# Head pairs and dense products in 64-row halves of the array, attention chunk by chunk, x turned up front

## The chip, the cores and the metric

The kernel runs on one core of a Trainium2 chip. The metric is the device time of one execution in microseconds. Three executions of the kernel before took 794.4, 798.03 and 798.63 us; the median is 798.03 us. Engine names follow the profile: PE is TensorE (PEld its weight loads), DVE is VectorE, ACT is ScalarE, POOL is GpSimd, SP is SyncE, whose queue issues every DMA here.

## The reference

One token matrix `x` of 2048 x 512 goes through two branches, and a gate mixes them:

```python
g = sigmoid((x * gate_w).sum(-1, keepdims=True))
# A: 32 heads of 16, causal window of 256
q, k, v = split(x @ wqkv)
scores = q k^T * 16**-0.5, masked to 0 <= i - j < 256
a = (softmax(scores) v) @ wo
# B: 512 -> 1792 -> 512
b = gelu_tanh(x @ w1 + b1) @ w2 + b2
return g * a + (1 - g) * b
```

## The kernel before

**Arithmetic.** Dense products keep fp32 accuracy with three passes. Each operand is split into a high part and a low remainder, and one product of 128 x 128 by 128 x 512 becomes three matmuls, high by high, high by low and low by high (`mm3`, L90 to L92). A score product uses one pass instead: the high and low parts of a head are stacked as extra rows of the contraction (48 rows for each of two heads, `load_stack`, L341 and L342), so that a single matmul sums the three terms.

**Tiles.** Tokens are cut in four tiles (chunks) `t` of 512. `x` arrives in 128-token blocks, is turned by four 128 x 128 transposes on PE (L198) and kept as `xt`. The query, key and value products (`qkv_qk`, `qkv_v`; 12 groups of 12 matmuls for each tile) are written to DRAM (`SQ`, `SK`, `SV`) and read back in the stacked layout (`att_load`). The other branch has 56 groups `u` of 12 matmuls (`x @ w1`, then `gelu`, L535 to L553) and 32 groups `y` of 21 matmuls (`@ w2`, L601). `final` multiplies the attention output by `wo`: 192 matmuls of full width at the end.

**Attention.** Heads go in 8 groups `g_` of 4, and keys in 16 blocks `kb` of 128. For each block and head there are two score products of up to 384 columns. The first (`att_max`, L377) feeds the row maximum on DVE (L382). The negated maxima are turned and put by POOL into spare rows of the query stack (`att_rows`, L402), so that the second product (`att_exp`, L417) comes out with the maximum subtracted; ACT takes its exponential (L429) and POOL cuts the window edges (L421, L424). Every four blocks, `att_pv` (L449) multiplies the probabilities by the values, with four heads side by side in 32-column quarters of the array.

**Order of the work.** PE, ACT, DVE and POOL run in the order in which the program is written. A small planner (`tick`, `after`, `need`) places the follow-up operations by estimated times. One unit of attention is one key block of four heads: four `att_max`, four `att_exp`, and a share of dense work of `STEP` = 2296 ns between them (`fill`), taken as single `mm3` triples. The unit loop goes head group by head group, 16 blocks each, with the maxima 8 units ahead of the exponentials (`LEAD`). Before it stand 117 us of planned dense work (`START`): three tiles of query, key and value products and part of the fourth. SP's order is not written out. It is arranged when the program is built: an issue whose inputs are ready can move ahead of those that wait.

Of the kernel before, what the change touches and what calls it, by code (L numbers as in the profile page):

```python
# [18 lines left out]
T = 512  # L19
# [5 lines left out]
NG = H // 4  # L25
SCALE = DH ** -0.5
NEG = -1e30
GC = 1.0 / 0.044715
GS = 0.7978845608028654 * 0.044715


@with_exitstack
def gated_mix(ctx: ExitStack, tc: tile.TileContext, x, wqkv, wo, w1, b1, w2, b2, gate_w, out):
# [21 lines left out]
    XT = [dr.tile([NC, 128, 2, T], F32, name=f"XT{t}") for t in range(NT)]  # L55
# [5 lines left out]

# [12 lines left out]
    own = cp.tile([128, 4], F32, name="own")  # L74
    nil = cp.tile([128, 1], F32, name="nil")
    nc.gpsimd.memset(nil, 0.0)
    nc.gpsimd.memset(own, 0.0)
    for k in (0, 1):
        nc.gpsimd.affine_select(out=own[96:104], in_=own[96:104], pattern=[[-2, 4]], compare_op=ALU.not_equal,
                                fill=1.0, base=-k, channel_multiplier=1)  # L80
    nms = cp.tile([128, RB, 32], F32R, name="nm")
    nc.gpsimd.memset(f32(nms), 0.0)
    vbuf = cp.tile([128, 2, NB * 68 + 16], F32, name="vbuf")
    nc.gpsimd.memset(vbuf[:, :, NB * 68:], 0.0)
# [8 lines left out]

# [23 lines left out]

    wk4 = wqkv.rearrange("(c p) f -> p c f", p=128)
    wt, raws = {}, {}

    def load_raw(key, early=False):
# [6 lines left out]
        if early and kind == "v":  # L128
            if i == 0:
                raws["v"] = f32(sb.tile([128, NC, 2, T], F32R, tag="xt", bufs=1, name="raw_v"))  # L130
            raw = raws["v"][:, i, 0]
        elif early:
            raw = sb.tile([128, 2, 384], F32, tag="pt", bufs=14, name=f"raw_{kind}{i}")
# [29 lines left out]

    qs = cp.tile([128, 2, S], F32R, name="qs")
    ks = cp.tile([128, 2, 2, S], F32R, name="ks")

    def clear_k(i):  # L170

        pr, n = divmod(i, 4)
        v = ks[:, pr].rearrange("p s c -> p (s c)")
        c = 2 * pr + n // 2
        nc.scalar.activation(v[:, n * 1024:(n + 1) * 1024], nil.broadcast_to([128, 1024]), AF.Identity,
                             bias=own[:, c:c + 1])

    xts, xrs = {}, {}

    def load_xr(t):  # L180
        for b in range(NB):
            xrs[t, b] = sb.tile([128, D], F32, tag=("tmp", "raw")[b // 3], bufs=3, name=f"xr{t}_{b}")
            nc.sync.dma_start(xrs[t, b], x[t * T + b * 128:t * T + (b + 1) * 128])

    def qkv_x(t, b):

        if b == 0:
            if t < NT - 1:
                v = (ks[:, 0], ks[:, 1], qs)[t].rearrange("p a c -> p (a c)")
                v = v.rearrange("p (c s t) -> p c s t", c=NC, s=2)  # L190
            else:
                v = sb.tile([128, NC, 2, T], F32R, tag="xt", bufs=1, name=f"xt{t}")
            xts[t] = v
        xt = xts[t]
        xr = xrs[t, b]
        p = ps.tile([128, NC, 128], F32, tag="sm", bufs=3, name=f"xp{t}_{b}")
        for c in range(NC):
            nc.tensor.transpose(p[:, c], xr[:, c * 128:(c + 1) * 128], ident)  # L198
        tick(4 * 110)

        def hi():
            nc.scalar.activation(xt[:, :, 0, b * 128:(b + 1) * 128], p, AF.Copy)

        def lo():
            nc.vector.tensor_sub(xt[:, :, 1, b * 128:(b + 1) * 128], p,
                                 f32(xt[:, :, 0, b * 128:(b + 1) * 128]))
            done.add(("x", t, b))
        after(100, hi), after(500, lo)

    def gate(t):  # L210
        for b in range(NB):
            after(1500 * b, gate_z, t, b)
        after(6500, gate_end, t)
# [8 lines left out]
    def gate_z(t, b):  # L222
        xr = xrs.pop((t, b))
        junk = sb.tile([128, D], BF16, tag="sq", bufs=2, name=f"xj{t}_{b}")
        nb = t * NB + b
        nc.vector.tensor_tensor_reduce(junk, xr, gwb, 1.0, 0.0, ALU.mult, ALU.add, z[:, nb:nb + 1])

    def qkv_qk(t, j):

        xt = xts[t]  # L230
        dst, i = (SQ[t], j) if j < NC else (SK[t], j - NC)
        w = wt["qk", j]
        p = ps.tile([128, T], F32, tag="d", bufs=2, name=f"qk{t}_{j}")
        for c in range(NC):
            mm3(p, w[:, 0, c], w[:, 1, c], xt[:, c, 0], xt[:, c, 1], c == 0, c == NC - 1)
            yield MM3
        e = sb.tile([128, 2, T], F32R, tag="h", bufs=8, name=f"qke{t}_{j}")

        h = 1 if j < NC else 0

        def hi():
            nc.scalar.activation(e[:, h], p, AF.Copy)  # L242

        def lo():
            nc.vector.tensor_sub(e[:, 1 - h], p, f32(e[:, h]))  # L245
            nc.sync.dma_start(dst[8 * i:8 * i + 8].rearrange("h d s c -> (h d) s c"), f32(e))
            done.add(("qk", t, j))
        after(100, hi), after(700, lo)

    def qkv_v(t, b):  # L250
        xt = xts[t]
        p = ps.tile([128, D], F32, tag="d", bufs=2, name=f"v{t}_{b}")
        ts = slice(b * 128, (b + 1) * 128)
        for c in range(NC):
            w = wt["v", c]
            mm3(p, xt[:, c, 0, ts], xt[:, c, 1, ts], w[:, 0], w[:, 1], c == 0, c == NC - 1)
            yield MM3
        vx = f32(sb.tile([128, 2, T], F32R, tag="h", bufs=8, name=f"vx{t}_{b}"))
        vx = vx.rearrange("p s t -> p (s t)")[:, 0:H * 17].rearrange("p (h c) -> p h c", c=17)
        nc.gpsimd.memset(vx[:, :, 16:17], 1.0)  # L260

        def ev():
# [3 lines left out]
        after(100, ev)  # L266

    def warm(n):

        p = ps.tile([128, T], F32, tag="d", bufs=2, name=f"warm{now[0]}")  # L270
# [4 lines left out]
    def qkv(t):  # L275
        last = t == NT - 1
        qk = [("qk", j) for i in range(NC) for j in (i, i + NC)]
        vs = [("v", b) for b in range(NB)]
        pieces = qk[:2] + vs + qk[2:] if last else qk + vs
        if t == 0:  # L280
            keys = qk + [("v", c) for c in range(NC)]
            load_xr(0)
            for key in keys[0:4]:
                load_raw(key, True)
            warm(WARM[0])
            for b in range(NB):
                qkv_x(0, b)
            warm(WARM[1])
            split(keys[0], nc.vector)
            split(keys[1], nc.vector)  # L290
            nc.sync.dma_start(gwb, gate_w.partition_broadcast(128))
        need(*[("x", t, b) for b in range(NB)])
        for n, (kind, j) in enumerate(pieces):
            if not last and XAT <= n < XAT + NC:
                nc.sync.dma_start(XT[t][n - XAT], f32(xts[t][:, n - XAT]))
# [460 lines left out]
```

## Time and profile before

| what | value |
|---|---|
| median of three executions | 798.03 us |
| span of the profiled execution | 795.8 us |
| instructions | 14526 |
| data moved by DMA | 139.66 MB, mean 175 GB/s |
| DMA packets | 97085, of them 32496 under 512 B |

The span runs from the first to the last instruction of the profiled execution, so some 2 us of the median lie around it. "Busy" of PE is the time in which a matmul is somewhere in the array; matmuls overlap, so the distance from start to start says what one costs, not its listed duration.

### The profile page before, as it was taken

To read this page: it belongs to the slowest core of one execution; us is meant where nothing else is said; L and a number is where in the kernel's file an instruction comes from. 1 tells how busy PE (TensorE), PEld (TensorE's weight loads), DVE (VectorE), ACT (ScalarE), POOL (GpSimd) and SP (SyncE) were. 2 spreads that over 40 slices of the span, in tenths; PEclk is the share of its full clock that TensorE was granted. 3 is DMA by queue.
4 is the path that set the end of the run, shared out by engine and by line. 5 is a ranking of instruction groups with operands and counts; after the bars stand their busy time and mean duration, and the time that the engine had idled before them with its cause. 6 is when DMAs were issued, how large, how long until landed. Compare 5 with 4: busy or idle time off the path is not lost.

```text
span 795.8 us, 14526 instructions
## 1 busy us (share of the span) xinstructions
PE 770.4 (97%) x4630; PEld 616.6 (77%) x4630; DVE 530.0 (67%) x1516; ACT 423.3 (53%) x865; POOL 363.7 (46%) x701
## 2 busy tenths in 40 slices
PE   8999999979999999999999989999999999999997
PEld 6888888866887778778778867788788787777676
DVE  5432333999578758956896799568668976891343
ACT  4433433365466546745764666457546754675540
POOL 2200000157447645854674477447645854675100
PEclk9999999999999999999999999999999999999999
DMA  9986756637443654664336656424664455255782
GB/s 296 354 300 207 300 185 211 205 100 269 135 114 91 222 153 128 196 180 112 99 108 170 179 142 204 126 84 124 201 189 126 138 193 163 68 154 161 259 281 93
DMA packets 97085, 139.66 MB, mean 175 GB/s; under 512 B 32496, under 2 KB 44016, under 8 KB 97008
## 3 DMA queue, kind: packets, MB, share of 16 engines
q1 hardware_dynamic: 97008, 138.72, 55.2%
q8 instruction: 37, 0.61, 0.3%
q14 instruction: 40, 0.33, 0.1%
HBM read 83.63 MB, written 55.05 MB: 174 GB/s over the span
## 4 chain that ended last, share of the span: by engine, by line
PE 78%; DVE 10%; issue 5%; DMA 3%; ACT 2%; POOL 2%; SPq 0%; DVEq 0%; POOLq 0%
PE pv L449 9%; PE st L417 9%; PE sm L377 8%; PE y L90 6%; PE y L92 6%; PE y L91 5%; PE u L90 4%; DVE jm L382 4%; PE u L91 4%; PE u L92 4%; PE qk L92 4%; PE qk L90 4%; PE qk L91 4%; PE v L90 2%; PE v L92 2%
## 5 line engine op out<-in xcount | busy, mean ns | idle before, releaser
L382 DVE CUSTOM_DVE_ANT_0 jm<-sm,mask 128x384 bf16<-128x384 f32 (+2 forms) x512 | 269.3, 526 | 117.7 <-PE sm L377 92.6
L429 ACT ACTIVATE pt<-st 128x384 f32<-128x384 f32 (+2 forms) x512 | 229.0, 472 | 132.3 <-PE st L417 127.8
L421 POOL TENSOR_SCALAR_AFFINE_SELECT pt<-pt 128x256 f32<-128x256 f32 x256 | 126.7, 495 | 190.2 <-ACT pt L429 184.6
L377 PE MATMUL sm<-ks,qs 96*128 96x384 f32 (+2 forms) x512 | 170.8, 335 | 12.2 <-DVE M L382 11.4
L417 PE MATMUL st<-qs,ks 128*128 128x384 f32 (+2 forms) x512 | 169.4, 333 | 2.2 <-POOL qs L402 1.9
L377 PEld LDWEIGHTS sm<-ks,qs 96*128 96x128 f32 x512 | 96.2, 188 | 41.2 <-DVE M L382 23.6
L417 PEld LDWEIGHTS st<-qs,ks 128*128 128x128 f32 x512 | 97.1, 190 | 21.8 <-POOL qs L402 3.6
L424 POOL TENSOR_SCALAR_AFFINE_SELECT pt<-pt 128x256 f32<-128x256 f32 x224 | 101.4, 453 | 0.0
L553 POOL TENSOR_TENSOR h<-x1h,h 128x512 fp32r<-128x512 f32 x56 | 73.0, 1304 | 38.1 <-DVE h L550 30.8
L92 PE MATMUL y<-w,h 128*128 128x512 f32 x224 | 88.1, 393 | 1.9 <-POOL h L553 1.9
L90 PE MATMUL y<-w,h 128*128 128x512 f32 x224 | 89.6, 400 | 0.0
L91 PE MATMUL y<-w,h 128*128 128x512 f32 x224 | 87.6, 391 | 0.0
L402 POOL CAST qs<-tt 8x256 fp32r<-8x256 f32 x128 | 64.0, 500 | 49.4 <-PE u L92 38.2
L449 PE MATMUL pv<-pt,vbuf 128*32 128x384 f32 (+2 forms) x1408 | 84.3, 386 | 0.1
L90 PE MATMUL u<-mx,w 128*128 128x512 f32 x196 | 79.1, 404 | 0.0
L91 PE MATMUL u<-mx,w 128*128 128x512 f32 x196 | 76.6, 391 | 0.0
L92 PE MATMUL u<-mx,w 128*128 128x512 f32 x196 | 76.5, 390 | 0.0
L449 PEld LDWEIGHTS pv<-pt,vbuf 128*32 128x32 f32 x1408 | 41.5, 110 | 42.0 <-issue 28.9
L544 ACT ACTIVATE sqh<-sqh 128x512 f32<-128x512 f32 x56 | 35.3, 631 | 64.2 <-DVE sqh L541 64.1
L541 DVE SCALAR_TENSOR_TENSOR sqh<-sqh,x1h 128x512 f32<-128x512 f32 x56 | 54.5, 974 | 1.9 <-ACT sqh L538 1.7
L245 DVE TENSOR_TENSOR qke<-qk,qke 128x512 fp32r<-128x512 f32 x32 | 22.1, 690 | 49.5 <-ACT qke L242 49.5
L92 PEld LDWEIGHTS y<-w,h 128*128 128x128 f32 x224 | 42.0, 188 | 13.1 <-POOL h L553 4.0
(116 smaller groups left out, 1189.6 us busy)
## 6 DMA issues: line engine op xcount, KB each, us to landing
mx<-XT SPq DMA_DIRECT2D x24, 512.0 KB
SQ<-qke SPq DMA_DIRECT2D x16, 512.0 KB
SK<-qke SPq DMA_DIRECT2D x16, 512.0 KB
qs<-SQ SPq DMA_DIRECT2D x64, 128.0 KB
ND<-nd SPq DMA_DIRECT2D x32, 256.0 KB
ks<-SK SPq DMA_DIRECT2D x60, 128.0 KB
raw_w<-in_B_w_dram SPq DMA_DIRECT2D x28, 256.0 KB
SV<-vx SPq DMA_DIRECT2D x16, 272.0 KB
```

Of the source, the lines that this page charges most:

```text
L90: nc.tensor.matmul(p, lh, rh, start=first, stop=False)
L91: nc.tensor.matmul(p, lh, rl, start=False, stop=False)
L92: nc.tensor.matmul(p, ll, rh, start=False, stop=last)
L377: nc.tensor.matmul(p[:, :w], qs[0:96, pr, b * 128:(b + 1) * 128], ks[0:96, pr, s, k0:k0 + w], start=True, stop=True)
L382: nc.vector.tensor_tensor_reduce(junk[:, :w], p[:, :w], mask[:, 384 - w:384], 1.0, -3e38, ALU.add, ALU.max, M[:, b % RB, i:i + 1])
L402: nc.gpsimd.tensor_copy(dst, tt[32 * i:32 * i + 8].unsqueeze(1).broadcast_to([8, 2, RB, 32]))
L417: nc.tensor.matmul(p[:, :w], ks[:, pr, s, kb * 128:(kb + 1) * 128], qs[:, pr, kb * 128:kb * 128 + w], start=True, stop=True)
L421: nc.gpsimd.affine_select(out=pt[:, :, 0:128], in_=pt[:, :, 0:128], pattern=[[0, 2], [1, 128]], compare_op=ALU.is_ge, fill=0.0, base=0, ch ...
L424: nc.gpsimd.affine_select(out=pt[:, :, 256:384], in_=pt[:, :, 256:384], pattern=[[0, 2], [-1, 128]], compare_op=ALU.is_ge, fill=0.0, base= ...
L429: nc.scalar.activation(pt[:, s, :w], p[:, :w], AF.Exp, scale=SCALE)
L449: nc.tensor.matmul(pv[32 * i:32 * i + 32, q - c * T:e - c * T], vt[:, 68 * (kb % NB) + 17 * i:68 * (kb % NB) + 17 * i + 32], pts[g_, kb, i ...
L553: nc.gpsimd.tensor_sub(h[:, 1], x1, f32(h[:, 0]))
```

## The change

1. **Halves for scores.** A head's stack now has `KR` = 56 rows (two copies of 16 values and 4 spare rows, and 16 rows for the low part) and begins at row 0 or row 64 of the array. The products of two heads are issued one after the other into different PSUM banks, one in the upper and one in the lower 64 rows.
2. **Halves for dense products.** From tile 1 of the query, key and value products to the last `y`, each matmul is cut in two of 64 rows. A group first runs all its upper halves, then all its lower halves; the lower halves of one group run beside the upper halves of the next (`chain`). Where a group passes from upper to lower, a no-op on PE waits for the last upper product, and at least two score calls must lie between (`apart`).
3. **Chunk by chunk.** Attention runs over pairs (chunk, head group), chunk first, with its own query and key tiles (`q`, `k`, three buffers each) that hold the 256 keys before the chunk as well. It begins after the first tile alone. `STEP` is 3050 ns, `LEAD` 6 units.
4. **x first.** All 16 blocks of `x` are loaded and turned during the first tile; tiles 2 and 3 go to DRAM in 128-column pieces at once.
5. **Spare rows through DRAM.** The constant rows (zeros for queries, the ones that select a head for keys) are no longer cleared in SBUF by ACT; `store_rows` writes them into `SQ` and `SK`, 8 DMAs for each of the 32 pairs.
6. **Buffers.** PSUM: 5 banks for scores (`sc`) and 3 for dense work, instead of 3 + 3 + 2.

```diff
+R = 20
+KR = 2 * R + 16
-    SQ = [dr.tile([H, 16, 2, T], F32, name=f"SQ{t}") for t in range(NT)]
-    SK = [dr.tile([H, 16, 2, T], F32, name=f"SK{t}") for t in range(NT)]
+    SQ = [dr.tile([H, R, 2, T], F32, name=f"SQ{t}") for t in range(NT)]
+    SK = dr.tile([H, R, 2, S], F32, name="SK")
...
+    def store_rows(zr, kr, t, g_):
+        hs = slice(4 * g_, 4 * g_ + 4)
+        for n in range(T // 128):
+            cs = slice(n * 128, (n + 1) * 128)
+            nc.sync.dma_start(SQ[t][hs, 16:R, :, cs].rearrange("h d s c -> h (d s) c"), zr)
+            cs = slice(t * T + n * 128, t * T + (n + 1) * 128)
+            nc.sync.dma_start(SK[hs, 16:R, :, cs].rearrange("h d s c -> h (d s) c"), kr)
...
+    def turn_x(k):
...
+            if t >= 2:
+                nc.sync.dma_start(XT[t][:, :, b * 128:(b + 1) * 128], f32(dst).rearrange("p c s t -> p (c s) t"))
...
+            if k + 6 < NT * NB:
+                load_xr(k + 6)
...
+    def first_tile():
...
+        for n, (kind, j) in enumerate(pieces(0)):
...
+            store_rows(zr, kr, n // NG, n % NG)
...
+            whole(qkv_qk(0, j) if kind == "qk" else qkv_v(0, j))
...
+            while n >= 3 and turned < NB + (n - 2) * 12 / 9 and turned < NT * NB:
+                turn_x(turned)
+                turned += 1
...
+        for c in range(NC):
+            store_x(1, c)
+        for u in range(12, NT * NG):
+            store_rows(zr, kr, u // NG, u % NG)
...
+    def half(group, k, r):
+        if group.p is None:
+            group.p = group.begin()
+        lhsT, rhs = group.mms[k]()
+        rows_ = slice(64 * r, 64 * r + 64)
+        n = 2 * len(group.mms)
+        if group.last and group.last[0] != r:
+            tc.add_manual_dep(nc.tensor.nop().ins, group.last[1].ins.name, SYNC, reason="the other half's bank")
+        ins = nc.tensor.matmul(group.p, lhsT[rows_], rhs[rows_], start=group.left == n, stop=group.left == 1,
+                               skip_group_check=True)
...
+    def att_load(i):
...
+        for s in range(2):
+            heads = slice(4 * g_ + s, 4 * g_ + 3 + s, 2)
+            load_stack(SK[heads, :, :, c * T - 256 + lo:(c + 1) * T], 0,
+                       lambda r, n: k[64 * s + r:64 * s + r + n, :, lo:])
+            load_stack(SQ[c][heads], 1, lambda r, n: q[64 * s + r:64 * s + r + n])
...
+    PARTS = [[(0, 0, 128), (1, 0, 256)], [(2, 0, 384)], [(3, 128, 384)], [(4, 256, 256), (5, 384, 128)]]
+    def att_exp(i, j, pr):
...
+        for kb, lo, w in PARTS[j]:
+            for s in range(2):
+                rows_ = slice(64 * s, 64 * s + KR)
+                nc.tensor.matmul(p[s][:, at:at + w], k[rows_, pr, kb * 128:(kb + 1) * 128], q[rows_, pr, lo:lo + w],
+                                 start=True, stop=True, skip_group_check=True)
+            at += w
...
+    first_tile()
+    NU = len(combos) * NB
+    att_load(0), att_load(1)
     for u in range(-LEAD, NU):
+        i, j = divmod(u, NB)
+        mi, mj = divmod(u + LEAD, NB)
+        if mj == LOADAT and mi > 0 and mi + 1 < len(combos):
+            att_load(mi + 1)
...
+        for pr in range(2):
+            if mi < len(combos):
+                att_max(mi, mj, pr)
+            fill(STEP / 4)
+            if i >= 0 and (j > 0 or combos[i][0] > 0):
+                att_exp(i, j, pr)
+            if i > 0 and j == PVAT and pr == 0:
+                att_pv(i - 1)
+            fill(STEP / 4)
```

More of the change, by code (lines that the diff above doesn't have):

```diff
@@ new lines, in half @@
+    def half(group, k, r):
[8 more added lines that the diff above has]
+                               skip_group_check=True)
+        group.last = r, ins
+        group.left -= 1
+        if group.left == 0:
+            after(100, group.end, group.p)
@@ L392, in att_rows @@
+    def att_rows(i):
+        need(*[("max", i, j, h) for j in range(RB) for h in range(4)])
+        m = Ms.pop(i)
         nm = nms[:, :, 0:8].rearrange("p b (i k) -> p k b i", k=2)
```

743 lines of the change are left out of this document (369 added, 374 removed).

## The prediction

> **What bounds the kernel now.** I read the page first: the engine totals, PE's row of the 40 slices and the DMA row.
>
> ```profile
> PE 770.4 (97%) x4630; PEld 616.6 (77%) x4630; DVE 530.0 (67%) x1516; ACT 423.3 (53%) x865; POOL 363.7 (46%) x701
> PE   8999999979999999999999989999999999999997
> DMA  9986756637443654664336656424664455255782
> ```
>
> PE has something in flight nearly always; nothing else is near its limit over the whole span. Then the busy time by stretch (columns: length, busy time and instructions of each engine, granted clock, DMA share, GB/s).
>
> ```profile
> 0.00:60.00 60.00, 57.93 (x260) 45.89 (x261) 26.89 (x51) 24.99 (x43) 10.59 (x29) 1.00 0.90 316
> 160.00:740.00 580.00, 563.59 (x3671) 448.81 (x3674) 436.42 (x1314) 344.21 (x734) 348.31 (x658) 1.00 0.50 150
> ```
>
> In the attention stretch PE idles 16 of 580 us at full clock, DVE works 75%. Only the first 60 us load the DMA engines, at 0.90. What a product costs is read from start to start in PE's timeline:
>
> ```profile
> 399.79 0.34 PE L377 MATMUL sm<-ks,qs 96*128 96x384 f32 x1
> 399.97 0.34 PE L417 MATMUL st<-qs,ks 128*128 128x384 f32 x1
> 400.14 0.39 PE L90 MATMUL u<-mx,w 128*128 128x512 f32 x1
> 400.37 0.39 PE L91 MATMUL u<-mx,w 128*128 128x512 f32 x1
> 400.60 0.39 PE L92 MATMUL u<-mx,w 128*128 128x512 f32 x1
> ```
>
> A score product takes 0.175 us, a dense one 0.23 us (I use 0.232). The chain of work that ended last gives the value products:
>
> ```profile
> 188.92 2.08 PE pv L449 x32
> 206.27 2.73 PE pv L449 x48
> ...
> 727.45 2.73 PE pv L449 x48
> ```
>
> The 32 chunks are (727.45 - 188.92) / 31 = 17.37 us apart. The order written out asks, per chunk, for 4 x (2.296 dense + 8 x 0.175) + 2.73 = 17.5 us. So PE's own instructions set the pace, and a change pays here by what it takes off PE.
>
> The whole before, as a check on these prices: first tile 45 us, 1776 dense matmuls after it x 0.232 = 412, 1024 score products 175 (a few are narrower), value products 24 x 2.73 + 8 x 2.08 = 82, and the end from the first `a` product:
>
> ```profile
> 742.40 0.50 PE L90 MATMUL a<-wo,ot 128*128 128x512 f32 x1
> ```
>
> 795.8 - 742.4 = 53.4 us. The sum is 768; 28 us are left for PE's waits and the passages into and out of the 32-column quarters. I carry these 28 us over.
>
> **The change, part by part.**
>
> *Scores in halves.* No row shows two row halves side by side, but the column quarters bear on it: 48 value products take 2.73 us, 0.057 each, and most have 256 or 384 columns, while a score product of 384 alone takes 0.175. So four products in separate parts of the array do overlap. I take one pair for the price of one, 0.175; the other end is two, 0.35. Maxima: 24 pairs of (chunk, group) have 8 head pairs, 33.6 us, and the 8 of chunk 0 have as many of which four are narrower, in all 8.6 us: 42. Exponentials: 240 head pairs x 0.175, and 0.016 for the second part of the 112 that are in two parts: 44. Together 86 us in place of 175: **89 us saved**.
>
> *Dense products in halves.* 1776 slots of two halves, and some 14 at the ends of the chain where one half is empty: 1790 x 0.232 = 415 us against 412. The no-op at each of 124 passages could cost, at the low end nothing: the last upper half ends 0.39 us after its start, its own slot is 0.23 and two score pairs of 0.175 stand between. The high end is 0.2 us each, 25 us, with all of PE's queue behind it and ACT and DVE for its products. I take nothing, the value of those rows. Value products stay at 82 us.
>
> *Weight loads.* They double for the dense part.
>
> ```profile
> 401.08 0.19 PEld L377 LDWEIGHTS sm<-ks,qs 96*128 96x128 f32 x1 [0.52 <-DVE M L382]
> 401.19 0.19 PEld L417 LDWEIGHTS st<-qs,ks 128*128 128x128 f32 x1
> ```
>
> Two follow at 0.11 us, and 96 rows take as long as 128. Two loads in turn need 0.22: inside a dense slot, but over the 0.175 of a score pair. That is a rival below. The Trainium skill, "TensorEngine Tiling (Array Packing)", Key Properties, says that tiles load weights and multiply in parallel; by it nothing is added. No run so far shows a 64-row load.
>
> *DVE.* Its work stays, in less time. The groups:
>
> ```profile
> L382 DVE CUSTOM_DVE_ANT_0 jm<-sm,mask 128x384 bf16<-128x384 f32 (+2 forms) x512 | 269.3, 526 | 117.7 <-PE sm L377 92.6
> L541 DVE SCALAR_TENSOR_TENSOR sqh<-sqh,x1h 128x512 f32<-128x512 f32 x56 | 54.5, 974 | 1.9 <-ACT sqh L538 1.7
> L547 DVE SCALAR_TENSOR_TENSOR x1h<-sqh,x1h 128x512 f32<-128x512 f32 x56 | 39.6, 706 | 1.8 <-POOL qs L402 1.1 <-ACT sqh L544 0.7
> L550 DVE CAST h<-x1h 128x512 fp32r<-128x512 f32 x56 | 26.0, 464 | 0.7
> ```
>
> A run of seven `u` groups (84 slots, 19.4 us) spans 8.5 units of 2.296 before and 6.4 units of 3.05 after; a unit then lasts 3.05 + 4 x 0.175 + 0.68 = 4.43 us, the run 28.3 us. DVE has 7 x 2.14 for gelu, 6.4 x 4 x 0.526 for maxima and some 1.6 for the rest: 30 us. That is 1.5 us too much in each of eight runs: **+11 us** (nothing if it slips into the `y` runs, 30 if each excess doubles). POOL gets 256 puts instead of 128:
>
> ```profile
> L402 POOL CAST qs<-tt 8x256 fp32r<-8x256 f32 x128 | 64.0, 500 | 49.4 <-PE u L92 38.2
> ```
>
> 64 us more on 348 busy of 580: hidden, since it still has a quarter of its time free; the loads of the next stacks (0.3 MB more for each pair of chunk and group) are hidden at a DMA share of 0.50. Without that cover both would hold `att_exp`.
>
> So everything between the first tile and `final` is 415 + 86 + 82 + 28 + 11 = 622 us.
>
> *When it can begin.* The first PE instruction after the first tile is `att_max`, which waits for `att_load(0)`; all dense halves are queued behind it on PE. In SP's program order 318 issues stand ahead of that load: 16 of `x`, 12 raw weights, the gate and the bias, 16 stores of `XT`, 4 + 8 of `SQ` and `SK` (keys now in two), 4 of `SV`, and **256 row stores**. What an issue costs, from SP's timeline:
>
> ```profile
> 443.60 0.42 SPq L341 DMA_DIRECT2D qs<-SQ  x1
> 444.08 0.43 SPq L342 DMA_DIRECT2D qs<-SQ  x1
> 444.55 0.42 SPq L341 DMA_DIRECT2D qs<-SQ  x1
> 445.01 0.43 SPq L342 DMA_DIRECT2D qs<-SQ  x1
> 445.54 0.38 SPq L364 DMA_DIRECT2D vbuf<-SV  x1
> ...
> 447.49 0.60 SPq L479 DMA_DIRECT2D den<-ND  x1
> 448.14 0.58 SPq L482 DMA_DIRECT2D num<-ND  x1
> ...
> 455.93 0.60 SPq L487 DMA_DIRECT2D rb<-RD  x1
> ```
>
> One every 0.47 us when they queue, whatever the size: `den` with 16 KB is no cheaper. The same shape of pattern as a row store (three dimensions on both sides) is that of `qs`, so I take 0.47: 318 x 0.47 = 149.5 us, plus 0.8 for the start. The load's own eight issues add 3.8, and landing takes
>
> ```profile
> 328.79 2.02 DMA ks<-SK
> ```
>
> 2.0 us. **Attention starts at 156 us.** The bounds of the issue: 0.37 (an issue of 0.32 and the step between) gives 124, 0.65 (0.60 and the step) gives 204 if the row stores alone are that dear. PE itself would be through the first tile at 8.45 + 144 x 0.2275 + 12 turns x 0.35 = 45 to 50 us:
>
> ```profile
> 8.45 0.50 PE L90 MATMUL qk<-ks,qk 128*128 128x512 f32 x1 [0.72 <-ACT qk L145]
> ...
> 25.56 0.60 PE L198 MATMUL xp<-ident,xr 128*128 128x128 f32 x4
> 25.91 0.48 PE L90 MATMUL qk<-ks,qk 128*128 128x512 f32 x1
> ```
>
> So PE waits over 100 us, which is more than the halves save. Before, three tiles of dense work covered the start.
>
> **Sum**, against the profiled execution: 156 + 622 + 53 = 831 us; with the 2 us that the median has beside the span, **833 us**.
>
> **The rivals.**
>
> *A. Row stores are dear issues.* `den`, `num` and `rb` take 0.58 to 0.60, and their DRAM side begins with a dimension of 8; the row stores begin with 4 heads. What speaks against it is that those three also meet 128 partitions on the other side, which a row store doesn't. At 0.65 for each of 256: 204 + 622 + 55 = 881 us. The Trainium skill, "DMA: Bandwidth & Descriptors", Why a DMA increments its semaphore by 16 and not by 1, says that a copy runs on the largest number of engines up to 16 that divides both outermost dimensions, and that the issuing sequencer itself writes what is then missing of the count of 16. By that a row store uses four engines and belongs with the 0.60 rows, whose copies would use eight. No row shows the engines of one copy.
>
> *B. The loads overtake the stores* (the other side). SP's order isn't program order:
>
> ```profile
> 24.80 0.45 SPq L304 DMA_DIRECT2D b1c<-in_B_b_dram  x1
> ...
> 32.69 0.42 SPq L588 DMA_DIRECT2D ya<-in_B_b_dram  x1
> ```
>
> `b1c` is written for the eleventh piece, about 36 us, `ya` for the other branch after 117 us; both were issued early, since they were ready. If `att_load(0)`, whose inputs are stored at about 20 us, goes ahead of the row stores that it doesn't need, attention starts at about 60 us, bounded by 19 MB at 316 GB/s: 60 + 622 + 55 = 737 us. Against it: the row stores are ready at the very start too, and earlier in the program. Each store overtaken is worth 0.47 us, so with 75 overtaken (or an issue at 0.36) the time equals before.
>
> *C. Weight loads of a pair go one after the other.* A score pair costs 0.22, one in two parts 0.44: 432 pairs x 0.045 and 112 second parts x 0.2 make 42 us more: 875 us. For it speaks only the 0.11 row.
>
> *D. Halves don't overlap.* 415 + 86 us more, some 1330 us. The value products speak against it.
>
> **How the numbers follow.** Forecast 0.36 (801 to 850 for its issue bounds and DVE), A 0.22, B 0.34, C 0.06, D 0.02. The forecast and B are close; the row of `qs` and the order of readiness decide for the first. Its own range is 800 to 888 with A. The range to hold 8 in 10 takes in B: 725 to 888, leaving out D, the no-op's high end on top of A, and B under 725. A measurement can tell 0.5% here, about 4 us. Faster: B and a little of the forecast's low end, 0.37. Same: 0.05. Slower: 0.58.
>
> **What would show it.** Right: PE's slices near 0 from about 50 to 150 us, SP with row stores without a break until then and `att_max` released by a load of `k` or `q`; row stores 0.47 us apart (A: 0.65); after that score pairs 0.175 apart and slots of 0.232 (C: 0.22; D: doubled), chunks 4 x 4.43 = 17.7 us apart, DVE the main releaser in runs of `u`. Wrong: a load of `q` among the first 60 us on SP; no gap in PE's row; or waits on `k` throughout, if eight issues and their landing don't fit into the two units (8.9 us) that `LOADAT` leaves.

## The result and the profile after

The changed kernel takes 1112.1 us (median of four runs, 1109.9 to 1113.9) against 797.5 us for the kernel before beside it: the ratio is 1.395, with an interval of 1.391 to 1.399. The prediction said 833 us, with a range of 725 to 888. It had the direction (slower, for the reason that PE waits at the start), and missed the size by 280 us.

The page of the profile after: engine totals, then PE, its granted clock, the DMA engines and their rate in 40 slices of 27.8 us.

```profile
span 1111.4 us, 19103 instructions
PE 786.6 (71%) x6598; PEld 645.2 (58%) x6598; DVE 530.2 (48%) x1516; ACT 399.9 (36%) x825; POOL 412.4 (37%) x828
PE   7343000004888787778988989899798899896988
PEclk9666555555989898788999999899989899999989
DMA  6545532226585566556655547456574565444463
GB/s 184 149 122 154 146 70 23 23 23 167 154 258 158 171 192 170 156 153 178 175 140 136 146 123 222 106 139 163 130 202 125 146 170 131 95 139 123 171 203 110
```

Two things are to be seen. PE stands still from slice 5 to 9 (111 to 250 us), and from 167 us on the DMA engines move only 23 GB/s: that is not a lack of bandwidth. And behind it PE's row holds 7s and 8s where before it held 9s, at a clock that often falls below full speed (mean 0.842, before 0.997).

The first score product, in PE's timeline, gives the first loss, and PE's waits from 290 to 1060 us (total, times, longest) the causes named for the second:

```profile
262.35 0.44 PE L582 MATMUL sm<-k,q 56*128 56x128 f32 x1 [156.52 <-DMA q<-SQ]
```

```profile
PE sm L582 <- DMA q<-SQ: 39.5, 16, 5.1
PE y L483 <- POOL h L395: 18.6, 9, 5.0
PE sm L582 <- DVE M L587: 12.5, 10, 4.3
PE st L627 <- ACT pt L641: 10.3, 12, 1.8
PE st L627 <- DVE M L587: 9.8, 15, 2.1
```

Attention starts at 262.4 us and not at 156: 106 us. From there to the end of the span it takes 1111.4 - 262.4 = 849 us and not 622 + 53 = 675: 174 us. The two make up the 280. In this second stretch PE's busy time, each 5 us weighted with the granted clock, is 675 us. That it equals the whole forecast for the stretch is chance, since 39 us of the forecast were for waits, passages and DVE. The 174 us beside it are 118 us in which PE idles and 56 us that the lower clock adds.

What was forecast of the array itself came true. PE's timeline in a stretch without waits:

```profile
501.55 0.39 PE L483 MATMUL u<-mx,w 64*128 64x512 f32 x1
501.55 0.39 PE L483 MATMUL u<-xt,w 64*128 64x512 f32 x1
501.78 0.39 PE L483 MATMUL u<-mx,w 64*128 64x512 f32 x1
501.79 0.39 PE L483 MATMUL u<-xt,w 64*128 64x512 f32 x1
...
502.70 0.34 PE L582 MATMUL sm<-k,q 56*128 56x384 f32 x2
502.88 0.39 PE L483 MATMUL u<-mx,w 64*128 64x512 f32 x1
```

Two dense halves of different groups start together and the next pair 0.23 us later. Two score products (x2) cost 0.18 us together. Their weight loads, in PEld's timeline of the same place, start together as well:

```profile
501.55 0.18 PEld L483 LDWEIGHTS u<-mx,w 64*128 64x128 f32 x1
501.55 0.18 PEld L483 LDWEIGHTS u<-xt,w 64*128 64x128 f32 x1
...
502.48 0.19 PEld L582 LDWEIGHTS sm<-k,q 56*128 56x128 f32 x2
```

So the halves run side by side, weight loads included, and the change does take work off PE. A measure of it is PE's busy time, each stretch of 10 us weighted with its granted clock, summed: 768.6 us before, 720.3 after. The 66 us between 786.6 busy and 720.3 are lost to the lower clock; 1111.4 - 786.6 = 325 us PE is idle.

### The profile page after: what moved, and what is told of

The parts are those of the page before. It is cut to its first block, busy times and chain, and to the rows that moved or that the text cites. A ratio compares the mean times of both kernels' runs of the same rounds, so it can differ in the third digit from the quotient of the medians.

```text
span 1111.4 us, 19103 instructions
## 1 busy us (share of the span) xinstructions
PE 786.6 (71%) x6598; PEld 645.2 (58%) x6598; DVE 530.2 (48%) x1516; ACT 399.9 (36%) x825; POOL 412.4 (37%) x828
## 4 chain that ended last, share of the span: by engine, by line
PE 37%; DMA 22%; SPq 19%; DVE 7%; POOL 7%; issue 5%; ACT 2%; DVEq 0%; POOLq 0%; ACTq 0%
PE y L483 10%; PE u L483 8%; SPq L136 7%; SPq L134 7%; DMA q<-SQ 7%; PE pv L661 5%; PE qk L483 4%; DVE jm L587 3%; PE st L627 3%; PE sm L582 3%; DMA RD<-den 3%; POOL q L608 3%; DMA k<-SK 3%; POOL pt L633 2%; DMA ND<-nd 2%
## 5 line engine op out<-in xcount | busy, mean ns | idle before, releaser
L641 ACT ACTIVATE pt<-st 128x384 f32<-128x384 f32 x480 | 208.8, 491 | 197.9 <-PE st L627 192.2
L582 PE MATMUL sm<-k,q 56*128 56x384 f32 (+2 forms) x512 | 124.7, 357 | 215.0 <-DMA q<-SQ 198.5
L483 PE MATMUL y<-w,h 64*128 64x512 f32 x1344 | 235.3, 422 | 24.1 <-POOL h L395 18.6
L483 PE MATMUL u<-mx,w 64*128 64x512 f32 x1176 | 202.2, 412 | 0.0
L608 POOL CAST q<-tt 8x256 fp32r<-8x256 f32 x256 | 114.6, 447 | 232.1 <-PE qk L483 166.4
L483 PEld LDWEIGHTS y<-w,h 64*128 64x128 f32 x1344 | 165.6, 200 | 44.3 <-POOL h L395 22.2
L483 PEld LDWEIGHTS u<-mx,w 64*128 64x128 f32 x1176 | 150.8, 196 | 7.6 <-issue 2.6
L627 PE MATMUL st<-q,k 56*128 56x256 f32 (+2 forms) x704 | 121.4, 314 | 26.5 <-ACT pt L641 10.3
L627 PEld LDWEIGHTS st<-q,k 56*128 56x128 f32 x704 | 94.4, 197 | 45.5 <-DVE M L587 15.8
L483 PE MATMUL qk<-xt,qk 64*128 64x512 f32 x576 | 103.5, 438 | 0.2
```

Source lines behind the costliest of these rows:

```text
L483: ins = nc.tensor.matmul(group.p, lhsT[rows_], rhs[rows_], start=group.left == n, stop=group.left == 1, skip_group_check=True)
L582: nc.tensor.matmul(p[:, :w], q[rows_, pr, j * 128:(j + 1) * 128], k[rows_, pr, at:at + w], start=True, stop=True)
L608: nc.gpsimd.tensor_copy(dst, tt[32 * a:32 * a + 8].unsqueeze(1).broadcast_to([8, 2, RB, 32]))
L627: nc.tensor.matmul(p[s][:, at:at + w], k[rows_, pr, kb * 128:(kb + 1) * 128], q[rows_, pr, lo:lo + w], start=True, stop=True, skip_group_c ...
L641: nc.scalar.activation(pt[:, s], p[s][:, :384], AF.Exp, scale=SCALE)
```

## The experiments

The theories at the beginning: (1) the row stores set the start, by the price of one issue or by the four engines that each may use; (2) the loads of the stacks come late throughout; against (2), that POOL and DVE, in their order, hold the scores up.

### Where the start went: row stores

SP's timeline of the changed kernel, first early, where SP has idled before each of these stores, then the first store behind the first tile, then in the gap:

```profile
11.62 0.24 SPq L134 DMA_DIRECT2D SQ<-zr  x1
12.51 0.24 SPq L136 DMA_DIRECT2D SK<-kr  x1
13.16 0.24 SPq L134 DMA_DIRECT2D SQ<-zr  x1
...
139.34 1.12 SPq L134 DMA_DIRECT2D SQ<-zr  x1
...
199.56 0.63 SPq L134 DMA_DIRECT2D SQ<-zr  x1
200.24 0.70 SPq L136 DMA_DIRECT2D SK<-kr  x1
200.98 0.67 SPq L134 DMA_DIRECT2D SQ<-zr  x1
201.69 0.67 SPq L136 DMA_DIRECT2D SK<-kr  x1
202.40 0.61 SPq L134 DMA_DIRECT2D SQ<-zr  x1
203.06 0.71 SPq L136 DMA_DIRECT2D SK<-kr  x1
...
255.71 0.72 SPq L136 DMA_DIRECT2D SK<-kr  x1
256.48 0.63 SPq L537 DMA_DIRECT2D k<-SK  x1
```

A row store is issued in 0.24 us where SP has idled before it, and six in a row from 15.58 us on come 0.34 to 0.41 us apart, so the issue as such is not dear. In the gap they come about every 0.71 us (a pair of stores, one for the queries and one for the keys, every 1.42: 200.98 - 199.56), and the loads of `k` stand behind the last of them. The windows of the gap (length, busy time of PE, PEld, DVE, ACT, POOL, clock, DMA share, GB/s):

```profile
150.00:200.00 50.00, 0.00 (x0) 0.00 (x0) 0.00 (x0) 0.00 (x0) 0.00 (x0) 0.50 0.21 23
200.00:250.00 50.00, 0.00 (x0) 0.00 (x0) 0.00 (x0) 0.00 (x0) 0.00 (x0) 0.50 0.20 23
```

Nothing but row stores runs, and the DMA share is 0.20 to 0.21: 3.3 of 16 engines. Each store has 4 heads outermost. `e1_rows_16_engines` writes the same bytes in as many stores, but each over 16 heads:

```diff
-        hs = slice(4 * g_, 4 * g_ + 4)
...
-            nc.sync.dma_start(SQ[t][hs, 16:R, :, cs].rearrange("h d s c -> h (d s) c"), zr)
...
+            hs = slice(16 * hh, 16 * hh + 16)
...
+            nc.sync.dma_start(SQ[t][hs, 16 + dd, s, cs], zr[:, dd])
```

> The 256 row stores keep their number and their bytes (16 KB each) but run over 16 heads, so that their outermost dimension is 16 in place of 4; only their shape changes. In the changed kernel a queued row store took 0.71 us on SP while the 16 DMA engines were busy for 0.21, about what four of them can give, and the first score product started at 262 us. Theory (four engines): a store is a matter of its engines, so with 16 of them SP issues one every 0.35 to 0.45 us, the first score product starts at 120 to 150 us and the time falls by about 125 us, to 970 to 1005 us. Rival (number of issues alone): 256 stores cost what they cost, start at 240 to 270 us, time 1090 to 1120 us.

Measured: 1055.6 us (ratio 1.325, 1.318 to 1.332), the first score product at 200.1 us. SP's timeline in this kernel's gap:

```profile
140.15 0.42 SPq L137 DMA_DIRECT2D SQ<-zr  x1
140.62 0.42 SPq L139 DMA_DIRECT2D SK<-kr  x1
141.08 0.42 SPq L137 DMA_DIRECT2D SQ<-zr  x1
141.54 0.42 SPq L139 DMA_DIRECT2D SK<-kr  x1
142.01 0.42 SPq L137 DMA_DIRECT2D SQ<-zr  x1
```

One every 0.465 us: just the price that the prediction took. With four heads it was 0.71. The start moved by 262.4 - 200.1 = 62 us, and the time by 56, between the two forecasts. The 160 stores that stand behind the first tile took 76 us (118.9 to 195.1) in place of 117 (139.3 to 256.5), 41 less. The other 20 or so came inside the tile, where stores stand between the loads that PE waits for. So both effects exist: with 16 heads SP's issue sets the pace, with four the engines do. A store of e1 also consists of 16 pieces of 1 KB and no longer of 32 of 512 B, so the run alone doesn't tell the heads from the size of the pieces. The single DMA packets in the two traces do. In the changed kernel, from 200 to 250 us, 283 packets of 4 B go beside the data of some 70 stores, four for each, and at no time is nothing in flight; it is one to four packets in all but 0.3 of the 50 us. In e1, from 150 to 190 us, there are 1372 such packets for some 86 stores, sixteen for each, and in 18 of these 40 us nothing is in flight. The Trainium skill, "DMA: Bandwidth & Descriptors", Why a DMA increments its semaphore by 16 and not by 1, has a copy run on the largest number of engines up to 16 that divides both outermost dimensions; the share of 3.3 engines and the four small packets of each store agree with four engines, the sixteen in e1 with 16.

`e2_rows_12_stores` writes the rows in 12 stores from 128 partitions.

```diff
-        hs = slice(4 * g_, 4 * g_ + 4)
...
-            nc.sync.dma_start(SQ[t][hs, 16:R, :, cs].rearrange("h d s c -> h (d s) c"), zr)
...
+            hs = slice(32 * m, 32 * m + 32)
+            nc.sync.dma_start(SQ[t][hs, 16:R].rearrange("h d s c -> h d (s c)"), zr.rearrange("p s c -> p (s c)"))
```

> The same rows are stored by 12 DMAs of 128 partitions in place of 256 of 4; nothing else changes. Theory (row stores hold the start): first score product at 65 to 85 us in place of 262, time 1111 - 187 = 925 us (905 to 945). Rival (the start is held by the bytes of the first tile, or by x loads that wait for each other): start over 120 us, time over 970. Either way the stretch after the start stays at some 790 us, since its loads are untouched.

Measured: 937.2 us (1.176, 1.169 to 1.183): **175 us of the loss** were the form of these stores. The first score product comes at 94.5 us, later than expected: the windows show 275 and 279 GB/s up to 90 us, so now the bytes seem to hold the start; e5 and e11 below, which bring fewer of them ahead of it, start earlier.

```profile
0.00:50.00 50.00, 35.61 (x145) 27.10 (x146) 26.29 (x51) 18.46 (x33) 10.52 (x20) 0.83 0.85 275
50.00:90.00 40.00, 16.27 (x75) 12.93 (x73) 7.61 (x19) 6.55 (x12) 0.61 (x4) 0.80 0.88 279
```

### Where the stretch went: loads, queues

In e2 PE still waits 65 us for `q` (22 of them once, at the start). `e3_stacks_48_rows` asks whether that is because a stack of 40 rows uses ten engines and not 16: it is e2 with `R` = 24, so 48 rows (and 20 stores). `e4_four_buffers` is e2 with four buffers for `q` and `k` and each load one pair earlier.

```diff
...
-        if mj == LOADAT and mi > 0 and mi + 1 < len(combos):
-            att_load(mi + 1)
+        if mj == LOADAT and mi > 0 and mi + 2 < len(combos):
+            att_load(mi + 2)
```

> As the run with 12 stores (here 20, since there are twice the rows), and each head keeps 8 spare rows in place of 4 (R = 24): the main part of a stack is 48 rows in place of 40, so that its load can be divided by 16 where 40 can only be divided by 10; 20% more bytes in it. Theory (loads of q and k come late because they run on too few engines): waits of the maxima for q fall from 39 us to under 15, the stretch of attention gets 40 to 90 us shorter than in the run with 12 stores, time 835 to 890 us. Rival (the stretch is long because POOL and DVE hold up the scores): within 15 us of the run with 12 stores, or slower by the bytes.

> As the run with 12 stores, with four buffers for q and for k in place of three and each load issued one pair of chunk and group (17.7 us) earlier; PT is 11 in place of 12 to make room. Theory (loads of q and k come late): waits for q vanish, the stretch of attention gets 60 to 120 us shorter than in the run with 12 stores, time 805 to 865 us. Rival (POOL and DVE hold up the scores): waits for q vanish too but others take their place, time within 30 us of the run with 12 stores.

e3: 963.4 us (1.209, 1.201 to 1.217), no less waiting for `q` (72 us); more engines do not bring the loads in time. The stacks also have 20% more bytes, so the number of engines alone was not tried. e4: 919.5 us (1.154, 1.148 to 1.160). The waits for `q` are gone but for the first, yet only 18 us came of it, since other waits took their place. PE's waits in e4:

```profile
PE sm L584 <- DVE M L589: 35.0, 11, 13.3
PE sm L584 <- DMA q<-SQ: 25.3, 2, 23.2
PE xp L218 <- DMA xr<-in_A_x_dram: 21.5, 6, 9.0
PE y L485 <- POOL h L397: 18.3, 9, 5.2
```

The longest, 13.3 us for a maximum, isn't a lack of DVE's time. DVE's timeline at that place, and then PE's:

```profile
175.15 0.69 DVE L281 TENSOR_TENSOR qke<-qk,qke 128x512 fp32r<-128x512 f32 x1
190.04 0.35 DVE L693 RECIPROCAL den<-den 128x32 f32<-128x32 f32 x1 [14.21 <-DMA den<-ND]
190.31 0.49 DVE L589 CUSTOM_DVE_ANT_0 jm<-sm,mask 128x384 bf16<-128x384 f32 x1
```

```profile
190.87 0.68 PE L584 MATMUL sm<-k,q 56*128 56x384 f32 x1 [13.33 <-DVE M L589]
...
191.35 0.62 PE L485 MATMUL qk<-xt,qk 64*128 64x512 f32 x1
191.47 0.62 PE L485 MATMUL v<-v,xt 64*128 64x512 f32 x1
191.78 0.62 PE L485 MATMUL qk<-xt,qk 64*128 64x512 f32 x1
...
196.67 2.15 PE L663 MATMUL pv<-pt,vbuf 128*32 128x384 f32 x32
```

DVE stands 14.2 us in front of a reciprocal whose operand a DMA hasn't brought, with the maxima queued behind it. And the wait has a second price: afterwards a slot takes 0.43 us (191.78 - 191.35), not 0.23, for 5.2 us (190.87 to 196.05), because the granted clock has fallen to half: it is 0.50 from 185 to 196 us and 0.92 in the two us behind. Long waits are paid twice. The Trainium skill, "TensorE: Matmul & The Clock Gate", Part 1: The HAM clock gate, has half speed after an idle window of about 3.4 us and full speed after a busy one of that length. The trace agrees on the two levels; here the way back took 5.2 us.

Four edits of e4, each alone, put the candidates to the test: the reciprocal due later, the spare rows out of the memory traffic, the 256 puts of POOL given to ACT, and the dense products whole again.

```diff
 e8:
-NORM = 4500
+NORM = 9000
 e5:
+    kst = cp.tile([128, 4, 2, T + 256], F32R, name="kst")
...
-        k = sb.tile([128, 2, T + 256], F32R, tag="k", bufs=4, name=f"k{i}")
+        k = kst[:, i % 4]
...
+            nc.sync.dma_start(f32(q[64 * s + 32:64 * s + 40]), ZD.rearrange("p (a c) -> p a c", a=2))
 e6:
-            nc.gpsimd.tensor_copy(dst, tt[32 * a:32 * a + 8].unsqueeze(1).broadcast_to([8, 2, RB, 32]))
+            nc.scalar.activation(dst, tt[32 * a:32 * a + 8].unsqueeze(1).broadcast_to([8, 2, RB, 32]), AF.Copy)
 e7:
-            for group, k, r in held.pop():
-                half(group, k, r)
+            mm_whole(*held.pop())
```

> As e4_four_buffers, with NORM 9000 in place of 4500, so that DVE's reciprocal of den, which waits for a load of ND, is due later. DVE idled 14.2 and 11.9 us at that reciprocal with the maxima queued behind it. If that is why PE waited 13.3 and 11.9 us for the maxima (DVE M), both go and the time is 885 to 902. If the stage of the qkv products is held by the stores and loads on SP anyway, another wait takes their place and the time stays over 908.

> As e4_four_buffers, but no spare row goes through memory: the ones in the stacks of the keys stay in four fixed buffers, written once (24 small copies), and the eight rows of the queries are zeroed by a copy of 32 KB (two more for each pair of chunk and group). Theory: the row stores' bytes are what is left of the late start, so the first score product moves from 98.8 us to 50 to 65, the stretch behind it stays at 819 +- 15, and the time is 870 to 895. Rival: turning all of x first (its loads and the stores of XT) holds the start; then the first score product stays past 80 us and the time is over 895.

> As e4_four_buffers, with the 256 puts of the maxima on ACT in place of POOL. If POOL's queue (puts that wait for DVE's turn, with gelu's low part behind them) is what stretches the MLP's part, PE's wait for POOL h falls from 18.3 us to under 5 and the time from 919.5 to 870 to 895. If DVE sets the pace there and POOL only follows, the time stays at 908 to 925.

> As e4_four_buffers, with the dense products of the chain whole (128 rows, one group after the other), and only the scores in halves. If halves of dense products cost and bring nothing, 905 to 930, with the same waits. If they hurt, because a group now takes two spans from its first product to its last and its result comes late, while three banks are held longer, under 895, with the waits for POOL h and for the maxima smaller.

- **e8** takes 901.5 us (1.132, 1.128 to 1.136), 18 less than e4. The wait for the maxima falls from 35.0 to 10.6 us. So one late load, in order ahead of the maxima, was worth 18 us.
- **e5** takes 866.9 us (1.090, 1.088 to 1.093), 53 less. The time is under what was expected, but by another way: the first score product comes at 83.2 us, not at 50 to 65, and the stretch behind it shrinks from 819 to 785 us, which neither theory had. Of these 34 us, 24.6 are PE's wait for the maxima (35.0 to 10.4): DVE waits 3.1 us for the loads of `den`, where it waited 31.1 in e4. So e5 and e8 win mostly the same wait in the stretch. That loads come sooner when less passes through memory fits this. But the main part of a stack is also loaded as 32 rows and not 40 in e5, and which of the two it is was not tried.
- **e6** takes 931.5 us (1.170, 1.167 to 1.173), 12 more, over both forecasts. The wait of `y` for POOL's `h` falls from 18.3 to 10.9 us, and that of `st` for ACT's `pt` rises from 9.4 to 33.4. The puts wait for DVE's turn of the maxima (`tt`) in either queue, 54.6 us on POOL in e4 and 29.2 us on ACT in e6, and hold up what is behind them; ACT is also busier (513 us for 400), and how much each of the two adds is not shown. Moving the blocking instructions to another engine only chose another victim.
- **e7** takes 959.5 us (1.206, 1.200 to 1.212), 40 more, over both forecasts, and the theory that halves of dense products bring nothing is wrong. It has fewer waits than e4; its PE is busy 868.8 us in place of 769.6. PE's timeline in e7 and then in e4 shows why:

```profile
609.59 0.44 PE L568 MATMUL sm<-k,q 56*128 56x384 f32 x2
609.96 0.96 PE L482 MATMUL u<-mx,w 128*128 128x512 f32 x3
610.85 0.44 PE L613 MATMUL st<-q,k 56*128 56x384 f32 x2
```

```profile
394.30 0.34 PE L584 MATMUL sm<-k,q 56*128 56x384 f32 x2
394.47 1.07 PE L485 MATMUL u<-mx,w 64*128 64x512 f32 x8
395.38 0.34 PE L629 MATMUL st<-q,k 56*128 56x384 f32 x2
```

In e4 a score pair costs 0.17 and four dense slots 0.91 = 4 x 0.23. In e7 the pair costs 0.37 and three whole products 0.89 = 3 x 0.23 + 0.20. A passage from instructions of 128 rows to ones of 64 and back costs 0.4 us, so 0.2 each on the average, and there are two for each score pair or two that stand together. The Trainium skill, "TensorEngine Tiling (Array Packing)", Key Properties, says that a change of the tiling mode drains the engine; e7 agrees, and gives the price. A dense slot costs 0.23 us either way, so the dense halves earn nothing by themselves. But without them the score halves lose more than they bring: PE's busy time weighted with the clock is 836 us in e7 and 722 in e4, against 769 in the kernel before.

Four edits of e5 followed. e9: gelu's cast from DVE to ACT, and its low part from POOL to DVE. e10: the maxima 8 units ahead in place of 6; the stacks are then loaded 4 units ahead of their first maximum and not 6. e11: tiles 2 and 3 of `x` turned during attention. e12: the 24 small copies that fill e5's fixed rows issued by ACT, and `NORM` 9000.

```diff
 e9:
-            nc.vector.tensor_copy(h[:, 0], x1)
+            nc.scalar.activation(h[:, 0], x1, AF.Copy)
-            nc.gpsimd.tensor_sub(h[:, 1], x1, f32(h[:, 0]))
+            nc.vector.tensor_sub(h[:, 1], x1, f32(h[:, 0]))
 e10:
-    att_load(0), att_load(1), att_load(2)
+    att_load(0), att_load(1)
...
-            att_load(mi + 2)
+            att_load(mi + 1)
...
-LEAD = 6
+LEAD = 8
...
-LOADAT = 2
+LOADAT = 0
 e11:
...
+        k_ = {-5: 8, -4: 9, -3: 10, -2: 11, 3: 12, 4: 13, 5: 14, 6: 15}.get(u)
+        if k_:
+            turn_x(k_)
```

> As e5_rows_kept, with gelu's cast of the high part on ACT in place of DVE and its low part on DVE in place of POOL (1.46 us there). If the late low part is what holds PE in the MLP's stage (17.4 us for POOL h in e5, and each wait brings a lower clock behind it), the wait goes to under 4 us and the time from 867 to 835 to 855. If DVE is the engine without room there, the maxima wait more (DVE M, 24 us in e5, over 35) and the time stays over 862.

> As e5_rows_kept, with the maxima 8 units ahead of the exponentials in place of 6, so four units in place of two lie between the last maximum of a pair and its first exponential, in which the turn and eight puts must pass DVE and POOL. If that way is too short, the waits of st for POOL q and DVE M (17 us in e5) go and the time is 840 to 858. If in-order queues of DVE and POOL are late as a whole, nothing changes: 860 to 875.

> As e5_rows_kept, but only tiles 0 and 1 of x are turned in the first tile; tiles 2 and 3 are turned in units -5 to -2 and 3 to 6 of the attention. If turning all of x first (2 MB of loads and 4 MB of stores ahead of att_load) holds the start at 83.2 us in e5, the first score product comes at 55 to 70 and the time is 845 to 860. If the small copies on SP hold it, the start stays past 75 and the time over 862.

> As e5_rows_kept, with the 24 small copies of the spare rows issued by ACT's queue in place of SP's (they took 18.7 us of SP there, with the loads of x behind them), and NORM 9000. If SP's order made the start late, the first score product comes at 60 to 72 and the time is 845 to 858. If the bytes do (some 18 MB ahead of it), the start stays past 78 and the time at 858 to 868.

| run | us | ratio, interval | first score product | reading |
|---|---|---|---|---|
| e9 | 846.1 | 1.064 (1.059 to 1.068) | 82.7 | 21 us less, as forecast; the wait for `h` from POOL (17.4) is gone, one of 6.3 for ACT's `h` has come |
| e10 | 857.4 | 1.077 (1.073 to 1.081) | 82.8 | 10 us less, in the range, but only in part by the way forecast: `st`'s wait for POOL's `q` (4.2) goes, that for DVE M stays (13.2 to 12.9), and that of `y` for POOL's `h` halves (9.0) |
| e11 | 868.6 | 1.092 (1.090 to 1.095) | 68.2 | the start is 15 us earlier and the time the same, against the forecast: the work is only moved |
| e12 | 861.3 | 1.082 (1.080 to 1.084) | 85.0 | not the start: PE now waits 20.4 us for ACT, whose queue issues the copies. The gain is elsewhere |

### Do the causes add up?

`e14_moves_together` is e5 with the edits of e9 and e10 (its loads too), with `NORM` 9000, and with the ones written in place by 16 short ACT instructions, no copies. `e15_dense_first` puts 120 slots of tile 1's dense work ahead of the first score product; `e13_x_late_too` adds e11's move of `x`.

```diff
+    for n in range(PRE):
+        apart[0] = 2
+        fill(12 * SLOT)
-STEP = 3050.0
+PRE = 10
+STEP = 2815.0
```

> As e5_rows_kept, with e9's move of gelu, e10's lead of 8 units and NORM 9000 together, and the ones of the spare rows written by 16 short ACT instructions in place of the 24 copies on SP. If waits add up, because each has a cause of its own: 867 less 21 (gelu), 10 (lead) and 10 to 15 (start at 62 to 72 in place of 83 us), so 818 to 832. If one in-order queue is behind them all, the gains overlap: 835 to 848.

> As e14_moves_together, with 120 slots of tile 1's dense products placed ahead of the first score product and STEP 2815, so that PE has work while the first stacks come. If the late start is what is left, PE's 18 us of waiting for q go and the time is 12 to 20 us under e14. If the shorter units leave DVE too little time for its maxima, the waits for DVE M take them back and the time is within 6 us of e14.

> As e15_dense_first, with the x of tiles 2 and 3 turned behind the first tile (four blocks among those dense products, four in the attention's first units). If the 6 MB that turning x first brings ahead of the first stacks still matter, 6 to 15 us under e15. If they are only moved (e11 gained nothing), within 5 us of e15.

e14 takes 813.4 us (1.023, 1.021 to 1.024), 53 less than e5 and a little under the forecast: 21 (e9) + 10 (e10) + 18 for the start, which moves from 83.2 to 65.6 us, are 49. SP's issue of the 24 copies had taken 18.7 us in e5, and e9 and e10 alone leave the start at 82.7 and 82.8, so the move of the start is that of the copies. The sum fits separate causes but doesn't prove them: `NORM` was not changed by itself in e5, and e11 started 15 us earlier without any gain. e15 takes 801.7 us (1.009, 1.007 to 1.012): from 60 to 110 us PE is busy 49.9 of 50, and the 12 us are as many as PE had waited for `q` in e14 (10.4 and 1.8). The units are also shorter (`STEP`), which was not tried alone. e13 takes 803.0 us (1.012, 1.006 to 1.017): turning `x` first costs nothing measurable once PE has other work.

The last three ask what e15 still loses in short waits. e16 takes 72 instructions off DVE for POOL (1516 to 1444), e17 has 72 slots ahead and not 120, with longer units, e18 is both.

> As e15_dense_first, with two things taken off DVE: the low part of every later weight (28 of 0.85 us) and of the first four or five gelu results of each turn (40 of 0.69 us) go to POOL, which is busy 43%; the last two of a turn, on which y waits, stay. If DVE's load is what makes the maxima and their turn late (sm and st waited 21 us for DVE M in e15), half of these waits go and the time is 786 to 797. If the waits come from the order of the queues, the time stays at 799 to 805.

> As e15_dense_first, with 72 slots ahead of the first score product in place of 120, and STEP 2885 in place of 2815. The first stacks are there at about 66 us, and 72 slots reach from 54.8 to 71.5 us, so PE still has no gap; units are 2.5% longer. If DVE limits in the units: 792 to 799. If not: 799 to 804.

> e16_less_dve and e17_dense_first_6 together. If DVE limits, 782 to 793, under the 795 of the kernel before; if not, 798 to 805.

e16: 808.6 us (1.015, 1.012 to 1.018), slower than e15 and over both forecasts, though the waits for DVE M fall from 20.8 to 16.4 us; e17: 800.5 us (1.006, 1.005 to 1.008); e18: 811.9 us (1.019, 1.017 to 1.021), also over both forecasts. DVE's load is not the limit; POOL's order is felt again (in e16 `y` waits 6.6 us for POOL, in e15 not at all). No version here beats the kernel before; the nearest, e17, is 0.6% slower.

## Why the prediction was wrong, step by step

| step, from the changed kernel on | us | took away |
|---|---|---|
| row stores: 12 in place of 256 (e2) | 937.2 | 175.0 |
| loads of the stacks one pair earlier (e4) | 919.5 | 17.6 |
| spare rows not through memory (e5) | 866.9 | 52.6 |
| gelu, lead, reciprocal, no copies (e14) | 813.4 | 53.5 |
| dense work ahead of the first scores (e17) | 800.5 | 12.9 |

What a step takes away depends on its place in this order: e8's reciprocal alone took 18 us from e4, most of which e5 takes as well.

- **Array.** Score pair 0.175, dense slot 0.232, weight loads in parallel: right, by the timelines above. Rivals C and D are refuted. The no-op shows no cost of its own in any view.
- **Order on SP.** All row stores ahead of `att_load(0)`: right, the line at 256.48 us shows it. Rival B is refuted.
- **Price of a row store.** This is the step that failed first: "The same shape of pattern as a row store ... is that of `qs`, so I take 0.47". It is 0.71, above the 0.65 of rival A as well: the 160 stores behind the first tile take 117 us, where 0.47 gives 75. That is 42 us. e1 shows it, with 0.465 over 16 heads. The row of `qs` gave the price of an issue, but the pace of these queues is the slower of the issue and the engines that a copy uses, four with 4 heads outermost and 16 with 16. Rival A's four engines were right; its 0.60, taken as issue time, was not.
- **The first tile.** "PE itself would be through the first tile ... 45 to 50 us": its last products end at 105, and SP's first 157 issues only at 139, so 0.88 us each and not 0.47, 65 us more. SP itself seldom waits there, 2.3 us at the most in one place, and is issuing for 127 of the 139 us: 96 row stores at 0.74 us each and 61 other copies at 0.91. It is PE that waits for SP: loads of `x` stand in SP's queue behind row stores (48.1 us of PE's waits are for them). The step to take the later of SP and PE was right; the price of an issue, read from the loads of `qs` with 128 KB, did not hold for the tile's other copies, nearly all of 256 or 512 KB. In e2, with 12 row stores, these take 0.99 us each. The kernel before had a sign of it in its own first 60 us: the 58 issues there take 0.61 us each on the average, and one, a store to `SK` at 27.10 us, takes 3.93. What makes them so dear in the changed kernel, at a DMA share of only 0.52 to 0.65, was not isolated. 65 + 42 are the 106 us of the start, within 1. With the stores and the copies out of the queue (e14) PE is through the tile at 55.
- **The 28 us carried over.** "I carry these 28 us over" and "**+11 us**" for DVE was the step that lost the other 174 us: the 39 us taken there stand against 118 us in which PE idles and 56 that the clock costs. In the kernel before, from 45 us on, PE idles 23 us and loses 1 to the clock. Before, PE's waits beyond the order written out were small (11.4 us for the maxima, 1.9 for POOL's `h`); they were a property of that order, not of the work. In the new order the loads of the stacks came late (the text named this as what would make it wrong: they have two units to land in), POOL's puts stood ahead of gelu's low part, and DVE's reciprocal ahead of the maxima. The words "hidden, since it still has a quarter of its time free" reasoned from POOL's share of busy time, where the order in its queue decided.
- **The clock.** The prediction has no term for it. The lower clock made 66 us of the 1112, 10 of them before the first score product, and as the waits went it went too: the mean clock is 0.842 in the changed kernel, 0.921 in e2, 0.935 in e5, 0.966 in e14.
- **What halves bring.** Forecast 89 less 3 us of PE's time; busy time weighted with the clock shows 48. Part of the difference can be how busy time is listed (a matmul before a pause counts to its end, 0.34 to 0.5 us, where its slot is 0.23); how much was not measured. The passages to the value products are no part of it: from the last score product to the first of them 0.26 us, and 0.20 back, by the median in both kernels.

Why the best version is no faster than before although its array works 47 us less (721.3 by the same measure): e17's PE is busy 741 of 799 us, so it idles 58, where the kernel before idled 25, and it loses 20 to the clock, where that lost 2. That gives back 51. Whether another order of DVE's, ACT's and POOL's queues would keep more of it was not found; e16 and e18, which move load from DVE to POOL, are slower.

## What to carry to other kernels

In these runs a queue of small DMAs was priced by the slower of two things, the issue and the engines that the copy's outermost dimension allowed, and everything behind it in that queue paid, not only what the new DMAs serve. Price an issue by copies of the same size and outermost dimension. When a change shortens PE's part of a balanced loop, don't carry the old waits over: list for each in-order queue which instruction would block, on what, and what stands behind it, since the share of busy time doesn't tell. And the score halves paid only while what ran between them was in halves too: count the passages first.

## What the runs showed of the hardware that was not expected

- A store of 16 KB with 4 heads outermost is paced at 0.71 us when queued (23 GB/s, 3.3 of 16 engines busy), at 0.465 with 16 heads, and its issue takes 0.24 us where SP has idled before it. Each such store has four packets of 4 B beside its data with 4 heads, sixteen with 16.
- A passage from 128-row to 64-row matmuls and back costs 0.4 us; products of 96 and 128 rows, in the kernel before, follow each other without one (0.175 and 0.23).
- Copies issued by ACT's queue block ACT as they block SP: in e12 the 24 copies took 21.9 us of ACT, and PE waited 19.7 us at one place for an ACT instruction behind them.
